# Seventy-four matmuls in the first eleven microseconds, and new scheduling constants from the end of layer 0's first pass on

## The chip, the cores and the metric

The kernel runs on one core of a Trainium2 chip. The metric is device time in microseconds for one execution, taken as the median of repeated runs. Four compute engines appear in the profile: PE (TensorE, matrix products; PEld is its weight load, which overlaps), DVE (VectorE), ACT (ScalarE) and POOL (GpSimd). SP (SyncE) issues the DMAs. Each engine works through its own list of instructions in order, and waits on semaphores for the others.

## The reference

Two layers, each a block of attention and a gated feed-forward block, with the same weights in both layers. Tokens S = 2048, model width D = 512, 32 heads of width 16, F = 1792; bfloat16 in and out.

```python
def _layernorm(x): return (x - mean(x)) / sqrt(var(x) + 1e-5)

def _A_ref(x, wqkv, wo):
    q, k, v = split_heads(x @ wqkv)              # 32 heads of 16
    p = softmax(q @ k^T * 16 ** -0.5)            # 2048 x 2048 for each head
    return merge_heads(p @ v) @ wo

def _B_ref(x, w_gate, w_up, w_down):
    return (gelu_tanh(x @ w_gate) * (x @ w_up)) @ w_down

x = A_x
x = x + _A_ref(_layernorm(x), A_wqkv, A_wo)
x = x + _B_ref(_layernorm(x), B_w_gate, B_w_up, B_w_down)
x = x + _A_ref(_layernorm(x), A_wqkv, A_wo)
x = x + _B_ref(_layernorm(x), B_w_gate, B_w_up, B_w_down)
```

## The kernel before

**Data.** All weights and the whole of x stay in SBUF. `X` is the residual in f32, 16 tiles of 128 tokens. `XNT` is the layer-normed x, transposed. `KT` holds the keys of four heads in each of 8 groups, head j on partitions 32j and up; `QT` holds queries the same way, `VP` the values with a column of ones, so that the sum of the softmax comes out of the same product as its numerator.

**Units.** The attention is cut into units: one group of four heads times a block of queries (512, in the last blocks of layer 1 also 256 or 128). A unit goes through two passes.

- Pass 1 (`p1_emit`, lines 1778 to 1816) finds the maximum of each row of scores. PE makes a tile of 128 queries by 512 keys in a PSUM bank (L1791), DVE reduces it to a maximum (L1806), one bank or two banks at a time. Some tiles are folded: PE multiplies the queries with the difference of two key blocks (L1610), ACT takes the positive part (L1617), and DVE adds and reduces in one operation (L1801), so that one DVE operation does for two tiles.
- Pass 2 (`p2_emit`, `p2_tile`, `pv_emit`) makes the scores again, transposed, with the negative maximum as an added row of `QT` (L1661). ACT takes the exponential (L1637), of one bank (128x512, called a single below) or of two (128x1024, a pair). PE then multiplies with `VP` (L1685) into bank 7, columns 0 to 271. After the last key tile ACT copies bank 7 out (L1238), and POOL or DVE normalizes.

4,096 tiles of scores go through each pass over the two layers.

**All else** (layer norms, projections, output projection, the feed-forward block; their matmuls are recorded at L717) is written as generators, "chains", which the planner steps between the matmuls of the two passes. While the gelu of a feed-forward block runs on ACT, no exponential is emitted, so that ACT changes its table only twice for a block.

**The planner.** The Python program that builds the kernel walks through simulated clocks, one for each engine (`emit`, `emit_pe`), and decides at each step which matmul PE gets next: pass 1, pass 2, a chain's step, a product of pass 2 with `VP`, or a "warm" matmul (L1830, 128x240 on zeros, into columns of bank 7 that nothing reads), which it puts in when PE's load over the last 3.4 us of its own clock falls below a bound. What it decides is a fixed list for each engine. On the chip nothing is reordered: an early or a late engine changes only how long the others wait.

**The constants.** Its decisions depend on 21 constants. They are set anew for each stretch of 16 steps of pass 1 (a step is two tiles) from the table `PLAN`, 132 rows long; a layer has 1,024 steps, so row 64 is the first of layer 1:

```python
if pos["p1"] >= STRETCH * stretch[0]:
    if stretch[0] < len(PLAN):
        SPC, SPLIT, S1C, S2C, OV, LIM, NT, P2B, LAG, LAGT, FL, GL, FX, AHD, DUE, DUEM, PIECE, GP, NPV, PB, OVF = PLAN[stretch[0]]
    stretch[0] += 1
```

For instance P2B says which banks pass 2 may take for a pair (none, 4 and 5, or 4 to 6), S1C and S2C how early the two passes are started ahead of DVE and ACT, PIECE how many matmuls of a chain go in at a time, and FL up to which lag of pass 2 tiles are folded.

**The start.** SP issues the loads: x tile 0, tiles 1 to 3, the key weights, the query weights, tiles 4 to 7, the value weights, tiles 8 to 11 and 12 to 15. POOL makes an identity matrix `IDN` (L548). DVE clears bank 7 (L558). Tiles 0 to 3 are normed by DVE, POOL and, for tile 3, ACT (`ln_fast`, `ln_a3`); each is then transposed on PE by four 128x128 matmuls with `IDN` (`transpose_tile`, L914) and copied to `XNT` by ACT (L732) or DVE (L734). Then come the first projections of the queries and keys (L717, written out by L732 and L734 and moved to `QT` and `KT` by DMA, L1072 and L1000), and with them the first tiles of pass 1. Tiles 8 to 15 are normed on ACT and POOL (`layernorm_act`): copy and sum (L886), squares (L893), normalization on POOL (L874).

```python
for i, tt in enumerate(tts):
    ...
    yield ("pe", [sk], [("XNT", tt)])
    transpose_tile(lambda ck, xs=xs: xs[:, ck * 128:(ck + 1) * 128], [sk], XNT[...], [("XNT", tt)], ...)
    xnt_rec[tt] = tag
    at["tr"] = i
```

**The end.** In the last block pass 1 is over before pass 2; the rest is exponentials, the products with `VP`, and the output projection and the feed-forward block of the last 128 tokens, of which the gated block of the 384 tokens before is partly beside it (L1363, L1389).

Of the kernel before, what the change touches and what calls it, by code (L numbers as in the profile page):

```python
# [81 lines left out]
    (0.1, 0.1, 0.55, 0.42, 0.1, -0.1, 2, 1, 70, 76, 13, 80, 0.7, 2.0, 10, 6, 2, 1, 6, 1, 0.2),  # L82
# [12 lines left out]
    (0.15, 0.1, 0.55, 0.42, 0.0, -0.05, 3, 0, 5, 76, -2, 80, 0.7, 2.0, 20, 10, 2, 1, 7, 3, 0.2),  # L95
    (0.3, 0.1, 0.55, 0.42, 0.3, -0.05, 1, 0, 30, 76, 8, 20, 0.3, 2.0, 0, 6, 1, 2, 9, 1, 0.0),
    (0.15, 0.1, 0.55, 0.42, 0.0, -0.05, 3, 0, 70, 76, -2, 80, 0.7, 2.0, 15, 2, 2, 4, 3, 4, 0.0),
    (0.2, 0.1, 0.55, 0.62, 0.3, -0.05, 1, 2, 30, 84, 8, 60, 0.3, 2.0, -5, 2, 4, 3, 9, 4, -0.05),
    (0.4, 0.4, 0.65, 0.62, 0.3, -0.05, 3, 2, 22, 76, 8, 60, 0.7, 3.5, 20, 6, 2, 4, 5, 1, 0.2),
    (0.35, 0.4, 0.65, 0.62, 0.3, -0.05, 3, 2, 22, 76, 8, 60, 0.7, 2.0, 20, 6, 2, 4, 5, 1, 0.2),  # L100
    (0.35, 0.15, 0.75, 0.12, 0.3, -0.1, 3, 0, 5, 84, 8, 60, 0.3, 1.0, 15, -6, 2, 3, 3, 1, 0.05),
    (0.2, 0.05, 0.55, 0.52, 0.3, 0.0, 2, 0, 30, 84, 8, 60, 0.3, 2.0, 0, 2, 4, 1, 7, 2, -0.05),
    (0.1, 0.05, 0.55, 0.42, 0.3, -0.05, 1, 1, 30, 100, 8, 40, 0.5, 2.0, 10, 14, 1, 2, 11, 3, -0.1),
    (0.1, 0.05, 0.55, 0.42, 0.3, -0.05, 1, 1, 30, 100, 8, 40, 0.5, 2.0, 10, 14, 1, 2, 11, 3, -0.1),
    (0.15, 0.1, 0.55, 0.42, 0.0, -0.05, 3, 0, 5, 76, -2, 80, 0.7, 2.0, 15, 10, 2, 1, 7, 3, 0.2),
    (0.15, 0.1, 0.55, 0.42, 0.0, -0.05, 3, 0, 5, 76, -2, 80, 0.7, 2.0, 15, 10, 2, 1, 7, 3, 0.2),
# [30 lines left out]
    (0.1, 0.2, 0.55, 0.52, 0.0, -0.05, 3, 0, 62, 76, -2, 80, 0.7, 2.0, 10, 2, 2, 1, 6, 3, 0.2),
    (0.1, 0.3, 0.45, 0.42, 0.1, 0.0, 2, 1, 14, 116, 13, 100, 0.3, 3.5, 0, 2, 2, 1, 7, 1, -0.05),
# [1935 lines left out]
```

## Time and profile before

| what | value |
|---|---|
| median of the runs | 2481.94 us (3 runs, 2481.69 to 2482.12) |
| the profiled execution | 2481.77 us, of which the span of its instructions 2480.0 us |
| PE busy | 2409.1 us, 97% of the span |
| DVE busy | 2382.1 us, 96% |
| ACT busy | 2331.1 us, 94% |
| POOL busy | 810.2 us, 33% |

The span runs from the first instruction to the last; 1.8 us of the execution lie outside it. Busy shares are means over stages: the first 62 us hold 10.5 us of DVE's idle time and the last 62 us hold 37.5 us, of 98 us in all. A busy PE is not PE at its peak, since warm matmuls count as work. Times in the text are counted from the start of the span.

### The profile page before, as it was taken

The page shows a single profiled execution, that of the slowest core. Times are in us where ns is not written, and L with a number is a line of the kernel's source. Part 1 is how long each engine was busy: PE and PEld are TensorE (multiplying, and loading weights), DVE is VectorE, ACT ScalarE, POOL GpSimd, SP SyncE. Part 2 cuts the span into 40 slices and gives each one's busy share as a digit, 9 for nine tenths or more (in the row PEclk, how much of TensorE's full clock was granted, in tenths as well). Part 3 has the DMA queues.
Part 4 walks back from the last instruction along what each step waited for, and adds up shares of the span by engine and source line. Part 5 has one row for each costly group of instructions (what it writes and reads, how often), then busy time and mean ns, then how long its engine had stood idle before and what let it go on. Part 6 is the DMA issues. An engine that isn't in the chain of part 4 may idle for free.

```text
span 2480.0 us, 69071 instructions
## 1 busy us (share of the span) xinstructions
PE 2409.1 (97%) x30004; PEld 1147.4 (46%) x30004; DVE 2382.1 (96%) x3173; ACT 2331.1 (94%) x3415; POOL 810.2 (33%) x1311
## 2 busy tenths in 40 slices
PE   8999999999999999999999999999999999999999
PEld 3444444444434454344434444434544345544655
DVE  8999999999999999999998999999999999999993
ACT  7999998999989999899989999989999999978987
POOL 5121125425433353521333131623116321333520
PEclk9999999999999999999999999999999999999999
DMA  3110000000000001000000000000000000000000
GB/s 94 44 57 15 2 15 12 2 2 15 13 12 2 4 11 23 6 14 11 11 10 2 9 15 5 10 16 8 4 13 15 2 10 3 14 10 12 13 8 10
DMA packets 64816, 34.32 MB, mean 14 GB/s; under 512 B 46848, under 2 KB 63488, under 8 KB 64512
## 3 DMA queue, kind: packets, MB, share of 16 engines
q1 hardware_dynamic: 64512, 29.90, 5.2%
q8 instruction: 235, 3.85, 0.6%
q14 instruction: 69, 0.57, 0.1%
HBM read 10.22 MB, written 2.10 MB: 5 GB/s over the span
## 4 chain that ended last, share of the span: by engine, by line
PE 47%; DVE 33%; ACT 19%; issue 1%; POOL 0%; ACTq 0%
DVE PM L1806 31%; ACT SCR L1637 17%; PE PS L1791 16%; PE PS L717 13%; PE PS L1685 10%; PE PS L1661 4%; PE PS L1830 4%; DVE SCR L1801 1%; ACT SCR L1617 1%; PE PS L1610 0%; PE PS L914 0%; ACT AO L1266 0%; ACT ACCS L1238 0%; ACT L1637 0%; DVE ST L769 0%
## 5 line engine op out<-in xcount | busy, mean ns | idle before, releaser
L1806 DVE TENSOR_REDUCE PM<-PS 128x1 f32<-128x512 f32 (+1 forms) x2507 | 2189.9, 935 | 47.6 <-PE PS L1661 25.1
L1637 ACT ACTIVATE SCR<-PS 128x512 bf16<-128x512 f32 (+1 forms) x2726 | 2005.9, 848 | 45.9 <-PE PS L1661 32.2
L1791 PE MATMUL PS<-KT,QT 32*128 32x512 bf16 x3894 | 1019.3, 384 | 41.3 <-DVE PM L1806 25.2
L1661 PE MATMUL PS<-QT,KT 32*128 32x512 bf16 (+2 forms) x5120 | 919.3, 340 | 2.6 <-ACT SCR L1637 1.7
L1685 PE MATMUL PS<-VP,SCR 128*128 128x51 bf16 (+1 forms) x16384 | 802.9, 187 | 10.1 <-ACT SCR L1637 5.3
L1685 PEld LDWEIGHTS PS<-VP,SCR 128*128 128x128 bf16 x16384 | 574.7, 96 | 473.4 <-issue 395.6
L1791 PEld LDWEIGHTS PS<-KT,QT 32*128 32x128 bf16 x3894 | 243.2, 91 | 526.3 <-DVE PM L1806 298.2
L1830 PE MATMUL PS<-WV,ZER 128*128 128x240 bf16 x2284 | 419.9, 265 | 3.9 <-ACT ACCS L1238 1.9
L1248 POOL TENSOR_TENSOR RL<-ACCS,CM 128x16 f32<-128x16 f32 (+2 forms) x71 | 182.2, 2567 | 485.2 <-ACT ACCS L1238 484.6
L1661 PEld LDWEIGHTS PS<-QT,KT 32*128 32x128 bf16 x5120 | 247.6, 91 | 73.9 <-ACT SCR L1637 44.3
L1830 PEld LDWEIGHTS PS<-WV,ZER 128*128 128x128 bf16 x2284 | 170.0, 96 | 70.0 <-issue 57.3
L1145 POOL TENSOR_TENSOR PM<-PM 128x16 f32<-128x16 f32 (+3 forms) x142 | 32.4, 228 | 425.0 <-DVE PM L1806 410.7
L1371 POOL TENSOR_TENSOR HT<-HT,AO 128x512 bf16<-128x512 bf16 x91 | 105.4, 1161 | 174.0 <-ACT AO L1369 174.0
L1408 POOL TENSOR_TENSOR KD<-KT 128x512 bf16<-128x512 bf16 x80 | 92.2, 1153 | 139.6 <-PE PS L1610 132.8
L1617 ACT ACTIVATE SCR<-PS 128x512 bf16<-128x512 f32 (+1 forms) x143 | 112.1, 787 | 26.3 <-PE PS L1610 25.3
L1801 DVE CUSTOM_DVE_ANT_0 SCR<-PS,SCR 128x512 bf16<-128x512 f32 x202 | 130.1, 686 | 3.2 <-PE PS L1661 1.2
L717 PE MATMUL PS<-XNT,WU 128*128 128x512 bf16 (+2 forms) x504 | 132.2, 357 | 0.0
L717 PE MATMUL PS<-WD,HT 128*128 128x512 bf16 x448 | 130.7, 381 | 0.0
L1268 POOL TENSOR_TENSOR X<-X,AO 128x512 f32<-128x512 f32 x47 | 59.5, 1266 | 199.2 <-ACT AO L1266 199.2
L717 PE MATMUL PS<-XNT,WG 128*128 128x512 bf16 (+2 forms) x504 | 119.9, 358 | 0.7 <-ACT HT L1353 0.7
L1353 ACT ACTIVATE HT<-PS 128x512 bf16<-128x512 f32 (+2 forms) x126 | 68.5, 550 | 43.1 <-PE PS L717 42.3
L717 PEld LDWEIGHTS PS<-XNT,WG 128*128 128x128 bf16 x504 | 37.6, 97 | 57.8 <-issue 33.2
(128 smaller groups left out, 1043.0 us busy)
## 6 DMA issues: line engine op xcount, KB each, us to landing
KT<-SG SPq DMA_DIRECT2D x64, 64.0 KB
QT<-MT SPq DMA_DIRECT2D x244, 1.0 KB
QT<-SG SPq DMA_DIRECT2D x56, 64.0 KB
out_dram<-AO SPq DMA_DIRECT2D x16, 128.0 KB, 1.7
WG<-in_B_w_gate_dram SPq DMA_DIRECT2D x4, 448.0 KB, 5.1
WU<-in_B_w_up_dram SPq DMA_DIRECT2D x4, 448.0 KB, 4.8
WD<-in_B_w_down_dram SPq DMA_DIRECT2D x4, 384.0 KB, 4.6
QT<-MT SPq DMA_DIRECT2D x68, 0.2 KB
```

The costliest lines, as they stand in the source:

```text
L717: ins = e.matmul(out_ap, lhsT=l, rhs=r_, start=(i == 0), stop=(i == n - 1))
L1248: emit("pool", lambda e: e.tensor_tensor(RL[:, s, 0:4 * nq], lsum, AP(CM1, 0, [[1, 128], [0, 4 * nq]]), op=ALU.pow), r=[("ACCS", s), ("CM1 ...
L1371: emit("pool", lambda e, ft=ft, o=o: e.tensor_tensor(HT[:, ft, c0:c0 + n], HT[:, ft, c0:c0 + n], AO[:, o, 0:n], op=ALU.mult), r=[("AO", o) ...
L1408: emit("pool", lambda e: e.tensor_tensor(KD[:, s, :], KT[:, g, ka * 512:(ka + 1) * 512], KT[:, g, kb * 512:(kb + 1) * 512], op=ALU.subtrac ...
L1617: emit("act", lambda e: e.activation(PT[:, s0:s0 + cnt, :], PS[:, bk:bk + cnt, :], ACTF.Relu), r=bks, w=[("PT", s0 + d) for d in range(cnt ...
L1637: emit("act", lambda e: e.activation(dst, src, ACTF.Exp, scale=DH ** -0.5), r=[BK[bk + i] for i in range(cnt)], w=[("PT", i) for i in slot ...
L1661: ins = e.matmul(bank(bk)[:, i * n:(i + 1) * n], lhsT=KT[32 * j:32 * j + 32, g, kt * 128:(kt + 1) * 128], rhs=QT[32 * j:32 * j + 32, s, 0: ...
L1685: ins = e.matmul(acc, lhsT=PT[:, slot, i * n + qt * 128:i * n + (qt + 1) * 128], rhs=AP(VP, (kt * H + 4 * g + j) * 17, [[NTT * H * 17, 128 ...
L1791: ins = e.matmul(bank(b), lhsT=QT[32 * j:32 * j + 32, s, qt * 128:(qt + 1) * 128], rhs=KT[32 * j:32 * j + 32, g, kb * 512:(kb + 1) * 512], ...
L1801: emit("dve", lambda e, i=i, b=b, sl=sl: e.tensor_tensor_reduce(PT[:, sl, :], bank(b), PT[:, sl, :], 1.0, -3.0e38, ALU.add, ALU.max, po[:, ...
L1806: emit("dve", lambda e: e.tensor_reduce(po, PS[:, bs[0]:bs[0] + cnt, :], axis=AX.X, op=ALU.max), r=bks, w=[("PM", sm) + h[1:] for h in hs] ...
L1830: return e.matmul(PS[:, b, NACC:512], lhsT=ZER[:, :], rhs=WV[:, 0, 0:512 - NACC], start=(b != 7), stop=(b != 7), skip_group_check=True)
```

## The change

Two things are changed.

First, a function `calm(n)` puts n matmuls on PE: 128x128, `IDN` times `IDN`, added to columns 272 to 399 of bank 7, which nothing reads. They are put into the list with `sch.op`, which records what they depend on (`IDN` is made, bank 7 is cleared) but moves none of the planner's clocks: the planner does not see them. 44 stand ahead of everything else on PE, then 11, 5, 9 and 5 behind the transposes of tiles 0, 1, 2 and 3.

Second, 53 of the last 72 rows of `PLAN` (between row 60 and row 130) hold other constants. Rows 0 to 59 stay. Row 128 is reached when pass 1 is over, rows 129 to 131 never.

```diff
@@ PLAN, from row 60 on (a few of the changed rows)
-    (0.1, 0.1, 0.55, 0.42, 0.1, -0.1, 2, 1, 70, 76, 13, 80, 0.7, 2.0, 10, 6, 2, 1, 6, 1, 0.2),
+    (0.1, 0.1, 0.55, 0.42, 0.1, -0.1, 2, 1, 70, 76, 13, 80, 0.7, 2.0, 10, 6, 2, 1, 5, 1, 0.1),
...
-    (0.35, 0.15, 0.75, 0.12, 0.3, -0.1, 3, 0, 5, 84, 8, 60, 0.3, 1.0, 15, -6, 2, 3, 3, 1, 0.05),
-    (0.2, 0.05, 0.55, 0.52, 0.3, 0.0, 2, 0, 30, 84, 8, 60, 0.3, 2.0, 0, 2, 4, 1, 7, 2, -0.05),
+    (0.15, 0.1, 0.55, 0.62, 0.3, -0.1, 1, 2, 22, 116, 8, 60, 0.3, 2.0, -5, 2, 4, 3, 9, 1, -0.05),
+    (0.15, 0.1, 0.55, 0.62, 0.3, -0.1, 1, 2, 22, 116, 8, 60, 0.3, 2.0, -5, -6, 4, 3, 9, 1, -0.05),
...
-    (0.1, 0.3, 0.45, 0.42, 0.1, 0.0, 2, 1, 14, 116, 13, 100, 0.3, 3.5, 0, 2, 2, 1, 7, 1, -0.05),
+    (0.2, 0.05, 0.75, 0.42, 0.3, -0.05, 2, 0, 30, 100, 8, 60, 0.3, 2.0, -5, 2, 4, 3, 7, 1, -0.05),
@@ _build(...)
-           ... T_TP=0.7, T_TPI=2.0, VL=0):
+           ... T_TP=0.7, T_TPI=2.0, VL=0, HC=(44, 11, 5, 9, 5)):
@@ behind the setup of KBIAS
+        def calm(n):
+            for _ in range(n):
+                sch.op("pe", lambda e: e.matmul(PS[:, 7, NACC:NACC + 128], lhsT=IDN[:, :], rhs=IDN[:, :],
+                                                start=False, stop=False, skip_group_check=True),
+                       r=[("IDN",)], w=[BK[7]])
+
+        calm(HC[0])
         filled = set()
@@ ln_to_xnt
                 xnt_rec[tt] = tag
                 at["tr"] = i
+                if tag == ("in", 0) and tts[0] == 0:
+                    calm(HC[i + 1])
```

In the two built programs the lists compare as follows. Apart from the 74, PE's list is the same up to the 1,923rd matmul of pass 1 of 3,894; DVE's up to its 1,517th reduction of 2,507, ACT's up to its 1,592nd exponential of 2,726.

| instruction | before | after |
|---|---|---|
| ACT exponential, pair / single (L1637) | 1370 / 1356 | 1394 / 1308 |
| ACT positive part of a fold, pair / single (L1617) | 59 / 84 | 58 / 88 |
| DVE reduction, two banks / one (L1806) | 1185 / 1322 | 1179 / 1330 |
| DVE add and reduce of a fold (L1801) | 202 | 204 |
| PE pass 1 / folds (L1791 / L1610) | 3894 / 202 | 3892 / 204 |
| PE warm matmuls (L1830) | 2284 | 2286 |
| PE silent matmuls | 0 | 74 |
| POOL memsets for folds, two columns / one (L1620) | 59 / 84 | 58 / 88 |
| SP DMAs | 667 | 667 |

All other instructions stand in both lists in the same number.

More of the change, by code (lines that the diff above doesn't have):

```diff
@@ L317, in _build @@
 def _build(nc, x_in, wqkv, wo, wg, wu, wd, out, layer_blocks=((512, 512, 512, 512), (512, 512, 512, 256, 128, 128)), ffn_groups=((512, 512, 512, 512), (512, 512, 512, 384, 128)),
[L318 removed]
+           n_ahead=6, n_pre=6, S1C=0.45, S2C=0.42, OV=0.3, PD=80, FDUE=20, LIM=-0.05, NT=1, AHD=2.0, DUEM=2, FDL2=0, OPD=12, URG=0.3, ft_tok=512, n_pt=8, n_qt=8, SPLIT=0.15, SPC=0.1, PVC=47, WARM=0.55, WARML=0.42, NPV=7, BOOST=0.0, LAG=62, LAGT=84, GP=2, SING=0, DUE=0, END=360, LAGE=10, FD=205, FDL=-10, QD=32, KD_=16, VD=20, FL=8, FMAX=6, NKD=2, FLOOK=2, FX=0.3, GF=1, NSPL=5, HSPL=0, TSPL=1, HNA=3, TNA=3, PB=1, OVF=0.0, FNP=1, NSG=3, LNT=8, HV=16, TW=0.95, HF=60, VS=14, SO=1.0, SF=1, SP=0, FAST=1, P2B=1, PIECE=2, GL=60, GLE=20, HARD=-1e9, VPARK=60, RUSH=1, XL=1000, NFE=2, NFA=6, LM1=0, T0=0.6, A3=1, DTX=2, DTA=2, T_TP=0.7, T_TPI=2.0, VL=0, HC=(44, 11, 5, 9, 5)):
     S = x_in.shape[1]
```

1 line of the change is left out of this document (removed), and 98 rows, old and new, of the table PLAN.

## The prediction

> **What bounds the kernel now.** I read the page's head and its chain of waits first, then the busy time of the engines in stretches, then the start and the tail as timelines.
>
> ```profile
> PE 2409.1 (97%) x30004; PEld 1147.4 (46%) x30004; DVE 2382.1 (96%) x3173; ACT 2331.1 (94%) x3415; POOL 810.2 (33%) x1311
> PE 47%; DVE 33%; ACT 19%; issue 1%; POOL 0%; ACTq 0%
> ```
>
> Three engines are full at once. PE's 97% holds warm matmuls, so it is the least certain of the three; DVE and ACT carry work that has to be done, and the chain changes hands between all three. So time can only go where DVE or ACT stands still, or where their own work shrinks. The built lists tell where the change acts at all: apart from the silent matmuls the first 1,923 pass 1 matmuls are in the old order, and the reordered places, found by counting pass 1 matmuls into the trace of before, are these stretches:
>
> ```profile
> core 0: us, PE busy (x) PEld busy (x) DVE busy (x) ACT busy (x) POOL busy (x), PEclk, DMA share, GB/s
> 1189.00:1209.00 20.00, 19.52 (x277) 10.09 (x274) 19.66 (x26) 19.84 (x22) 2.58 (x7) 1.00 0.05 10
> 1479.00:1549.00 70.00, 68.37 (x904) 34.87 (x901) 68.95 (x105) 69.24 (x79) 12.91 (x28) 1.00 0.02 4
> 1618.00:1658.00 40.00, 38.89 (x273) 12.96 (x272) 39.67 (x66) 32.24 (x52) 12.22 (x35) 1.00 0.06 12
> 1846.00:1924.00 78.00, 75.67 (x933) 36.22 (x929) 77.29 (x107) 74.07 (x112) 44.68 (x72) 1.00 0.11 22
> 1968.00:2061.00 93.00, 91.22 (x1134) 41.18 (x1130) 91.71 (x111) 89.42 (x156) 26.36 (x34) 1.00 0.02 8
> 2178.00:2197.00 19.00, 18.61 (x107) 6.31 (x104) 18.98 (x20) 8.00 (x14) 4.91 (x12) 1.00 0.05 10
> 2249.00:2315.00 66.00, 64.02 (x946) 32.72 (x945) 63.55 (x80) 60.65 (x98) 20.48 (x45) 1.00 0.04 12
> 2391.00:2427.00 36.00, 34.30 (x404) 17.91 (x403) 34.70 (x50) 26.03 (x42) 4.82 (x9) 1.00 0.03 5
> ```
>
> The third pair of numbers is DVE. It is idle for 0.34 + 1.05 + 0.33 + 0.71 + 1.29 + 0.02 + 2.45 + 1.30 = 7.49 us in these 422 us. That is all that a better order could win from DVE there. The kernel's larger idle stretches (the start, and the tail behind 2427 us) are looked at below.
>
> **The change part by part: the silent matmuls.** The start, by the timeline:
>
> ```profile
> 1.10 0.29 POOL L548 TENSOR_SCALAR_AFFINE_SELECT IDN<-HT 128x128 bf16<-128x128 bf16 x1
> 0.97 0.48 DVE L558 MEMSET PS<- 128x512 f32 x1 [0.97 <-PEq L2059]
> 3.91 2.53 SPq L508 DMA_DIRECT2D HT<-in_A_x_dram  x2
> 6.45 0.61 PE L914 MATMUL PS<-IDN,XN 128*128 128x128 bf16 x4 [6.45 <-DVE XN L790]
> 11.24 1.86 PE L717 MATMUL PS<-XNT,WQ 128*128 128x512 bf16 x4 [0.56 <-issue]
> 13.14 0.60 ACT L732 ACTIVATE SG<-PS 128x512 bf16<-128x512 f32 x1 [3.25 <-PE PS L717]
> 13.64 0.62 ACT L886 ACTIVATE X<-HT 128x512 f32<-128x512 bf16 x1
> 14.85 0.69 DVE L734 CAST SG<-PS 128x512 bf16<-128x512 f32 x1 [1.70 <-PE PS L717]
> 16.32 1.42 PEld L717 LDWEIGHTS PS<-XNT,WQ 128*128 128x128 bf16 x7 [0.28 <-issue]
> 20.16 1.82 DVE L1806 TENSOR_REDUCE PM<-PS 128x2 f32<-128x1024 f32 x2
> 30.53 3.01 POOL L874 TENSOR_SCALAR ATT<-HT,ACCS 128x512 bf16<-128x512 bf16 x4 [0.18 <-POOL ACCS L900]
> 33.92 6.71 DVE L1806 TENSOR_REDUCE PM<-PS 128x2 f32<-128x1024 f32 x8 [3.02 <-PE PS L1791]
> ```
>
> The column of the granted clock says 1.00 all along, but the pace doubles: the four query matmuls take 1.86 us, (1.86 - 0.17) / 4, some 0.43 us each, while from 16.32 us seven weight loads follow each other in 1.42 us, 0.20 us apart. PE is slow until it has worked without a break for 5 us.
>
> Can the 44 run in the gap? They need `IDN` (1.10 + 0.29 = 1.39 us) and bank 7 (0.97 + 0.48 = 1.45 us). At the slow pace 128 columns take a quarter of 0.43, 0.107 us, so they end at 1.45 + 44 x 0.107 = 6.16 us, 0.29 us ahead of the first transposes at 6.45. Bounds: if they follow each other as slowly as the four transposes on the mean (0.61 / 4 = 0.152), they end at 8.14 and the transposes are 1.7 us late. The other 30 stand in gaps between the transposes. Of the two I take the 0.107, since the four transposes include one latency at their end.
>
> What a fast PE wins: four transposes at 0.39 in place of 0.61 (the 0.39 is the row of the same four at 18.07 us, below) twice on the path, 0.4 us, the four query matmuls 4 x 0.21 = 0.9, the four key matmuls 0.9. ACT could write out the query projection at 13.14 - 1.3 = 11.8, DVE the key projection at 14.85 - 2.2 = 12.7, and the first reductions come some 2.2 to 2.7 us sooner.
>
> ```profile
> 18.07 0.39 PE L914 MATMUL PS<-IDN,XN 128*128 128x128 bf16 x4
> HT<-in_A_x_dram SPq DMA_DIRECT2D x2, 512.0 KB, 9.5
> 28.21 0.77 POOL L874 TENSOR_SCALAR ATT<-HT,ACCS 128x512 bf16<-128x512 bf16 x1 [0.37 <-ACT ATT L893]
> 20.00:22.00 2.00, 2.00 (x18) 1.31 (x17) 2.00 (x4) 2.00 (x7) 0.87 (x2) 1.00 0.46 98
> 26.00:28.00 2.00, 1.88 (x9) 0.43 (x8) 2.00 (x4) 2.00 (x8) 1.52 (x2) 1.00 0.03 8
> ```
>
> What is late next: at 33.92 us DVE stands still for 3.02 us in any case, waiting for keys of tiles 8 to 15, which come through ACT's copies and squares (from 13.64 on) and POOL's normalization (28.21, which waits for ACT, to 33.54). And the first of these copies cannot start sooner than its data: issued at 3.91, landed 9.5 us later, at 13.4. ACT has no gap from there to the normalization (its busy time, the fourth number, is 2.00 of 2.00 us in these two windows as in those between). So of the 2.2 to 2.7 us ACT's chain wins 13.64 - 13.4 = 0.2 us; the rest becomes a longer wait of DVE before 33.92. I take **-0.2 us**. Ends: -2.7 (if the wait at 33.92 shortened as well), and above zero +0.7, the 1.7 us of late transposes less the 1.0 us or more that the fast matmuls behind them give back.
>
> [...]
>
> **The new constants.** The durations by form:
>
> ```profile
> L1637 ACT ACTIVATE SCR<-PS 128x1024 bf16<-128x1024 f32 x1370 | 1297.9, 1074 | 20.6 <-PE PS L1661 14.7
> L1637 ACT ACTIVATE SCR<-PS 128x512 bf16<-128x512 f32 x1356 | 726.6, 619 | 25.3 <-PE PS L1661 17.5
> L1617 ACT ACTIVATE SCR<-PS 128x1024 bf16<-128x1024 f32 x59 | 62.1, 1059 | 2.0 <-PE PS L1610 1.6 <-DVE PM L1801 0.4
> L1617 ACT ACTIVATE SCR<-PS 128x512 bf16<-128x512 f32 x84 | 50.1, 597 | 24.2 <-PE PS L1610 23.7
> L1806 DVE TENSOR_REDUCE PM<-PS 128x2 f32<-128x1024 f32 x1185 | 1433.6, 1218 | 35.2 <-PE PS L1661 18.1 <-PE PS L1791 5.9 <-PE PS L1610 0.2
> L1806 DVE TENSOR_REDUCE PM<-PS 128x1 f32<-128x512 f32 x1322 | 887.5, 681 | 12.3 <-PE PS L1661 7.1 <-PE PS L1791 1.3
> L1801 DVE CUSTOM_DVE_ANT_0 SCR<-PS,SCR 128x512 bf16<-128x512 f32 x202 | 130.1, 686 | 3.2 <-PE PS L1661 1.2 <-PE PS L1791 0.6 <-PE PS L1610 0.2
> L1801 DVE DVE_READ_ACCUMULATOR2_ANT PM<- 128x1 f32 x202 | 16.7, 83 | 0.0
> ```
>
> ACT: 48 single exponentials become 24 pairs, 24 x (2 x 0.619 - 1.074) = 3.9 us less; the folds' positive parts cost 4 x 0.597 - 1.059 = 1.3 us more; together 2.6 us less. DVE: 8 x 0.681 - 6 x 1.218 + 2 x (0.686 + 0.083) = -0.3 us, which is nothing. PE: two more warm matmuls, in idle time. POOL's memsets and its moved key difference, and SP's moved DMAs (two transposes of the attention output go ahead of two query moves, three groups of query moves and one store of the output change places) lie on engines that are a third busy or wait most of the time; without that cover a moved query transfer would hold up its unit by one issue, and no group of these is larger than four.
>
> Of the new pairs seven fall at about 2058 us, seven at about 2298 and two net behind 2424. Is ACT the one that DVE waits for there?
>
> ```profile
> DVE PM L1806 <- PE PS L1661: 5.2, 20, 0.4
> DVE PM L1806 <- PE PS L1791: 0.7, 2, 0.5
> ```
>
> Between 2178 and 2427 us DVE's reductions wait 5.2 us for a PE that stands in front of a pass 2 matmul, so for a bank that ACT has not emptied. There a shorter exponential helps DVE. I let the 2.1 us that ACT saves outside the tail pass through and round: **-2.0 us** for 1189 to 2427. The far ends: -7.5, all idle time of DVE in the eight stretches; and above, +8: if all 422 us ran at the idle share of the worst of them, 2249 to 2315 (2.45 of 66, 3.7%), DVE would be idle for 15.6 us in place of 7.5.
>
> The tail, behind the last pass 1 work, is ACT's:
>
> ```profile
> 2421.80 5.83 ACT L1637 ACTIVATE SCR<-PS 128x512 bf16<-128x512 f32 x10
> 2438.19 7.54 ACT L1637 ACTIVATE SCR<-PS 128x1024 bf16<-128x1024 f32 x8
> ```
>
> A single takes 0.58 us here, a pair 0.94. Behind the last gelu the old list has 20 singles and 30 pairs, the new one 16 and 32: 2 x (2 x 0.58 - 0.94) = 0.4 us less. 272 pass 2 matmuls in place of 276 are left behind the last matmul of pass 1, one tile. Together **-0.5 us**, ends 0 and -1.0. The new list ends in more singles (six singles and three pairs for the last twelve tiles, before two and five), which costs 0.4 us at the very end if PE is ready; it is in the count.
>
> Sum: -0.2 - 2.0 - 0.5 = -2.7. The profiled execution took 2481.77, so 2479.1; the median of the runs lies 0.17 above it: **2479.2 us**, 0.11% less.
>
> **The rivals.**
> 1. *Nothing.* DVE is full wherever the order changes (98.2% of the 422 us), ACT's savings become ACT's waits: within 0.5 us of 2481.9. For it: the idle shares; against: the 20 waits on pass 2.
> 2. *The new order fills DVE's idle time.* 5.5 of the 7.5 us, with start and tail as above: 2481.9 - 6.2 = 2475.7. For it: the waits there are short and many (20 of at most 0.4 us), as a wrong order leaves them. Against: in half of the stretches there is under 0.8 us to win.
> 3. *The start passes through.* 2.7 us sooner at the first reductions and all later: 2479.2 - 2.5 = 2476.7. Against: the landing at 13.4 us. [...]
> 4. *Slower: a pair keeps two banks for longer.* The pass 1 matmul or chain step behind it on PE waits for both halves: 1.074 - 0.619 = 0.46 us later for each of 24 pairs, 10.9 us at most. Nothing shows beside the savings until a quarter of them hold up DVE (2.7 us), and it is slower by over 0.2%, about what a measurement of this kernel tells from no change (5.0 us), from 17 of them on. With 20: +9.1 - 2.7, 2488. Against: the kernel has 1370 pairs as it is, and its reductions wait 18.1 + 7.1 us for pass 2 over all 2480 us. The bound of +8 above gives about the same.
>
> **How the numbers follow.** Forecast (2477 to 2481): 0.46. Nothing: 0.22. Filled: 0.17. Start: 0.06, half of it beyond 2477. Slower: 0.09. So faster by over 0.2% 0.17 + 0.03 = 0.20, slower 0.09, within 0.71. The range leaves out rival 4 and the deep end of rival 2 (0.05): 2475 to 2484. The likeliest case alone is 2477 to 2481.
>
> **What would show it.** In the new profile: PE busy from 1.5 us on, the four query matmuls in about 1.0 us in place of 1.86 and ACT's write-out at about 12 us; ACT's first copy of tile 8 still at 13.4 us and a wait of DVE before 33.7 us of more than 4 us. Busy ACT 2.6 us less. DVE's reductions at about 2295 us 2 us sooner, their waits on pass 2 behind 2178 us down to some 3 us; the last pass 2 work 2.7 us sooner. I am wrong if the reductions at 34 us come 1 us or more sooner (the start passes through), or if they come later than 33.9, or if a stretch of the eight grows.

## The result, and the profile after

The changed kernel takes 2477.28 us (median of 16 runs, 2476.78 to 2478.8), the kernel before, timed beside it, 2481.94 us (16 runs, 2480.72 to 2482.69). The ratio is 0.9982, with an interval of 0.9975 to 0.999: 4.66 us or 0.19% less, a small gain that the interval tells from none. The profiled execution took 2477.07 us, its span 2475.3 us, 4.7 us less than before. In some executions (e4, e6 and e8 below) the granted clock falls to 0.50 for one stretch of 3.4 us, which costs 1.3 to 1.4 us; where a profile below holds such a stretch, it is said.

Line numbers have moved: by 7 between the lines 570 and 970 of before (L717 is now L724), by 9 behind that (L1806 is L1815, L1637 is L1646, L1661 is L1670). The silent matmuls are L572.

The page of the changed kernel, its head and the first line of its chain:

```profile
span 2475.3 us, 69012 instructions
PE 2387.4 (96%) x29880; PEld 1152.7 (47%) x30080; DVE 2381.7 (96%) x3179; ACT 2328.4 (94%) x3394; POOL 810.3 (33%) x1314
PE 48%; DVE 32%; ACT 19%; issue 1%; POOL 0%; DMA 0%; ACTq 0%
```

DVE has as much work as before, ACT 2.7 us less. (PE's 30,080 weight loads stand beside 29,880 matmuls: 200 matmul records are missing from this trace, so PE's busy time is not to be compared.) The start of the changed kernel, as a timeline (start, duration, then the idle time before and what ended it):

```profile
1.54 4.85 PE L572 MATMUL PS<-IDN 128*128 128x128 bf16 x44 [1.54 <-DVE PS L558]
6.10 0.41 DVE L797 TENSOR_SCALAR XN<-SCR,MV,LNS 128x512 bf16<-128x512 bf16 x1
6.57 0.47 PE L921 MATMUL PS<-IDN,XN 128*128 128x128 bf16 x4 [0.18 <-DVE XN L797]
11.34 0.81 PE L724 MATMUL PS<-XNT,WQ 128*128 128x512 bf16 x3 [0.50 <-issue]
11.98 1.03 PE L724 MATMUL PS<-XNT,WK 128*128 128x512 bf16 x4
12.18 0.60 ACT L739 ACTIVATE SG<-PS 128x512 bf16<-128x512 f32 x1 [2.38 <-PE PS L724]
12.68 0.62 ACT L893 ACTIVATE X<-HT 128x512 f32<-128x512 bf16 x1
HT<-in_A_x_dram SPq DMA_DIRECT2D x2, 512.0 KB, 8.8
17.53 1.81 DVE L1815 TENSOR_REDUCE PM<-PS 128x2 f32<-128x1024 f32 x2
31.66 4.99 DVE L1815 TENSOR_REDUCE PM<-PS 128x2 f32<-128x1024 f32 x6 [3.09 <-PE PS L1800]
```

The 44 end at 6.39 us and the transposes start at 6.57, right behind the normalization that they wait for anyway. The projections run at the fast pace (four key matmuls in 1.03 us). The first reductions come at 17.53 (before 20.16), and those at 33.92 now come at 31.66 us, with a wait of 3.09 us ahead of them, which was 3.02.

The eight reordered stretches of the changed kernel, each shifted by the lead that it has there (the columns are those of the table for before):

```profile
1189.00:1209.00 20.00, 19.18 (x278) 10.31 (x277) 19.94 (x27) 19.84 (x23) 0.86 (x1) 1.00 0.03 7
1476.00:1546.00 70.00, 67.46 (x903) 34.32 (x899) 69.55 (x106) 69.70 (x80) 13.45 (x31) 1.00 0.02 4
1615.00:1655.00 40.00, 39.06 (x269) 13.02 (x273) 39.71 (x66) 32.01 (x51) 12.38 (x35) 1.00 0.07 15
1843.00:1921.00 78.00, 75.91 (x931) 37.10 (x935) 77.19 (x113) 74.99 (x113) 44.72 (x75) 1.00 0.11 21
1966.00:2059.00 93.00, 89.82 (x1136) 42.16 (x1145) 91.77 (x112) 88.55 (x148) 26.35 (x34) 1.00 0.03 7
2176.00:2195.00 19.00, 18.34 (x92) 5.97 (x91) 18.89 (x19) 8.13 (x13) 3.77 (x9) 1.00 0.02 3
2247.00:2313.00 66.00, 64.13 (x965) 32.68 (x971) 64.07 (x81) 60.21 (x84) 22.18 (x50) 1.00 0.05 13
2387.00:2423.00 36.00, 34.49 (x411) 18.34 (x412) 34.74 (x50) 26.25 (x39) 4.82 (x9) 1.00 0.04 6
```

DVE is idle for 0.06 + 0.45 + 0.29 + 0.81 + 1.23 + 0.11 + 1.93 + 1.26 = 6.14 us here, 1.35 less than before, and nearly half of that is in the second stretch (1.05 to 0.45). Its waits from 2174 to 2423 us (total, times, longest), and ACT's two forms of exponential and the last of them:

```profile
DVE PM L1815 <- PE PS L1670: 4.5, 17, 0.4
DVE PM L1815 <- PE PS L1800: 1.0, 3, 0.5
...
L1646 ACT ACTIVATE SCR<-PS 128x1024 bf16<-128x1024 f32 x1394 | 1321.8, 1079 | 22.5 <-PE PS L1670 17.0
L1646 ACT ACTIVATE SCR<-PS 128x512 bf16<-128x512 f32 x1308 | 702.2, 622 | 23.1 <-PE PS L1670 16.1
...
2448.29 5.87 ACT L1646 ACTIVATE SCR<-PS 128x512 bf16<-128x512 f32 x9
```

The last exponential ends at 2448.29 + 5.87 = 2454.16 us; before it ended at 2459.02. Between the two ends, the lead over the kernel before can be followed by counting: the time at which the n-th of the 4,096 pass 1 tiles is reduced on DVE, in us against before. Both tiles of a fold are counted, since the two lists have their folds at different places.

| landmark | before | after | silent alone (e1) | silent, three rows (e10) | silent, rows from 92 (e6) |
|---|---|---|---|---|---|
| 18th tile | 35.1 | -2.3 | -2.3 | -2.4 | -2.4 |
| 1984th | 1151.2 | -2.2 | -2.3 | -2.5 | -2.3 |
| 2496th | 1477.3 | -2.3 | -2.3 | -2.5 | -2.3 |
| 2640th | 1554.9 | -3.2 | -2.2 | -3.3 | -2.3 |
| 3136th | 1838.2 | -3.3 | -2.3 | -3.3 | -2.3 |
| 3360th | 1958.8 | -3.6 | -2.3 | -3.3 | -2.6 |
| 3744th | 2195.4 | -3.6 | -2.2 | -3.3 | -1.2 (behind a stretch of slow clock) |
| 3920th | 2312.1 | -4.1 | -2.2 | -3.3 | -1.6 |
| last of pass 1 | 2426.9 | -4.1 | -2.2 | -3.3 | -1.7 |
| last exponential | 2459.0 | -4.9 | -2.2 | -3.3 | -2.4 |
| span | 2480.0 | -4.7 | -2.2 | -3.3 | -2.2 |

So the 4.7 us are 2.3 from the first 35 us, 0.9 from the stretch at 1480 to 1550, 0.4 from there to 1960, 0.5 from 2195 to 2312, and 0.6 from the tail. The lead grows where the order differs, and is kept in between.

### The profile page after: what moved, and what is told of

It reads as the page before. It is cut to its first block, busy times and chain, and to the rows that moved or that the text cites. A ratio compares the mean times of both kernels' runs of the same rounds, so it can differ in the third digit from the quotient of the medians.

```text
span 2475.3 us, 69012 instructions
## 1 busy us (share of the span) xinstructions
PE 2387.4 (96%) x29880; PEld 1152.7 (47%) x30080; DVE 2381.7 (96%) x3179; ACT 2328.4 (94%) x3394; POOL 810.3 (33%) x1314
## 4 chain that ended last, share of the span: by engine, by line
PE 48%; DVE 32%; ACT 19%; issue 1%; POOL 0%; DMA 0%; ACTq 0%
DVE PM L1815 30%; ACT SCR L1646 17%; PE PS L1800 15%; PE PS L724 13%; PE PS L1694 11%; PE PS L1670 4%; PE PS L1839 4%; DVE SCR L1810 1%; ACT SCR L1626 1%; PE PS L1619 0%; ACT AO L1275 0%; PE PS L921 0%; ACT AO L1378 0%; ACT L1646 0%; ACT HT L1362 0%
## 5 line engine op out<-in xcount | busy, mean ns | idle before, releaser
L1815 DVE TENSOR_REDUCE PM<-PS 128x1 f32<-128x512 f32 (+1 forms) x2509 | 2188.7, 934 | 47.0 <-PE PS L1670 24.0
L1646 ACT ACTIVATE SCR<-PS 128x1024 bf16<-128x1024 f32 (+1 forms) x2702 | 2003.7, 858 | 45.6 <-PE PS L1670 33.0
L1670 PE MATMUL PS<-QT,KT 32*128 32x512 bf16 (+2 forms) x5120 | 915.8, 340 | 3.3 <-ACT SCR L1646 2.1
L1670 PEld LDWEIGHTS PS<-QT,KT 32*128 32x128 bf16 x5120 | 246.8, 91 | 76.7 <-ACT SCR L1646 47.4
L1626 ACT ACTIVATE SCR<-PS 128x512 bf16<-128x512 f32 (+1 forms) x146 | 113.7, 782 | 26.8 <-PE PS L1619 26.0
L724 PE MATMUL PS<-XNT,WU 128*128 128x512 bf16 (+2 forms) x449 | 120.3, 354 | 5.8 <-issue 3.7
L724 PE MATMUL PS<-WD,HT 128*128 128x512 bf16 x387 | 116.3, 380 | 6.5 <-issue 4.9
L724 PE MATMUL PS<-XNT,WG 128*128 128x512 bf16 (+2 forms) x490 | 116.3, 357 | 2.4 <-issue 1.4
L724 PEld LDWEIGHTS PS<-XNT,WG 128*128 128x128 bf16 x504 | 37.7, 97 | 58.2 <-issue 32.9
```

The costliest lines, as they stand in the source:

```text
L724: ins = e.matmul(out_ap, lhsT=l, rhs=r_, start=(i == 0), stop=(i == n - 1))
L1626: emit("act", lambda e: e.activation(PT[:, s0:s0 + cnt, :], PS[:, bk:bk + cnt, :], ACTF.Relu), r=bks, w=[("PT", s0 + d) for d in range(cnt ...
L1646: emit("act", lambda e: e.activation(dst, src, ACTF.Exp, scale=DH ** -0.5), r=[BK[bk + i] for i in range(cnt)], w=[("PT", i) for i in slot ...
L1670: ins = e.matmul(bank(bk)[:, i * n:(i + 1) * n], lhsT=KT[32 * j:32 * j + 32, g, kt * 128:(kt + 1) * 128], rhs=QT[32 * j:32 * j + 32, s, 0: ...
L1815: emit("dve", lambda e: e.tensor_reduce(po, PS[:, bs[0]:bs[0] + cnt, :], axis=AX.X, op=ALU.max), r=bks, w=[("PM", sm) + h[1:] for h in hs] ...
```

## The experiments

**e1: the silent matmuls alone.** Does the start pass through?

```diff
 the changed kernel, with all of PLAN as before
-    (0.1, 0.1, 0.55, 0.42, 0.1, -0.1, 2, 1, 70, 76, 13, 80, 0.7, 2.0, 10, 6, 2, 1, 5, 1, 0.1),
+    (0.1, 0.1, 0.55, 0.42, 0.1, -0.1, 2, 1, 70, 76, 13, 80, 0.7, 2.0, 10, 6, 2, 1, 6, 1, 0.2),
...
```

> The 74 silent matmuls with the old constants; the work of every engine is else in the old order. Theory of the prediction (A: ACT's copies of x tiles 8 to 15 set the reductions at 33.9 us): 0.2 to 1.0 us sooner than before, since ACT's first copy came at 12.68 in place of 13.64 in the changed kernel. Rival (B: the first reductions set it, through PE's fixed order): the 2.3 us that the changed kernel showed at 34 us belong to this part alone, so span 2480.0 - 2.3 = 2477.7, constant from 34 us to the end.

Measured: 2479.88 us (11 runs, 2479.53 to 2481.41) against 2481.48 (33 runs, 2480.53 to 2482.83), ratio 0.9995 [0.9987, 1.0004]; span 2477.8, 2.2 less. The timeline of e1:

```profile
12.65 0.63 ACT L893 ACTIVATE X<-HT 128x512 f32<-128x512 bf16 x1
31.65 4.99 DVE L1815 TENSOR_REDUCE PM<-PS 128x2 f32<-128x1024 f32 x6 [3.12 <-PE PS L1800]
```

What follows: the reductions of 33.92 are 2.3 us sooner, and the table shows the lead kept, at -2.2, to the last instruction. Nothing behind 34 us waits for a fixed time. The silent matmuls are worth 2.2 us in this trace and 1.6 in the medians. The medians alone would not settle it, since their interval includes 1.

**e2: the constants alone.**

```diff
 the changed kernel, without calm
-        calm(HC[0])
-                if tag == ("in", 0) and tts[0] == 0:
-                    calm(HC[i + 1])
```

> The new constants without the silent matmuls. If the two parts add up, span 2480.0 - 2.4 = 2477.6 (the prediction had -2.5 for this part): nothing gained before 1190 us, 1.1 us by 1850 us, the largest step between 2270 and 2430 us. If the constants only pay with the earlier start, less than 1 us.

Measured: 2478.70 us (11 runs, 2478.04 to 2480.58), ratio 0.999 [0.9981, 0.9999]; span 2476.5, 3.5 less. In this execution PE became fast some 2 us sooner than in the profiled execution of before, though nothing was changed there, and its first reductions come at 19.08 us against 20.16. That lead of 1.1 us stays until 1230 us. So the constants win 3.5 - 1.1 = 2.4 us in the traces, 2.8 in the medians. With e1: 2.2 + 2.4 = 4.6 of 4.7 us by traces, 1.6 + 2.8 = 4.4 of 4.66 by medians. The two parts add.

**e3: only the 44 silent matmuls ahead, none in the gaps.** Are the other 30 needed?

```diff
-HC=(44, 11, 5, 9, 5)
+HC=(44, 0, 0, 0, 0)        (and PLAN as before)
```

> Old constants, the 44 matmuls ahead of the first transposes alone, without the 30 between the transposes. If the 44 open the clock and the transposes and projections keep it open: like the 74, span 2477.7. If the clock closes in the gaps between the transposes: the four query matmuls at some 0.43 us each again, first reduction at about 20 us, span 2479.5 to 2480.

Measured: 2481.59 us (10 runs, 2480.88 to 2482.46), 1.0001 [0.9992, 1.001]; span 2479.2. The stretches of e3 (columns as above; the last three are the granted clock, the DMA share and GB/s), and the query matmuls in its timeline:

```profile
4.50:7.80 3.30, 1.46 (x23) 1.11 (x22) 3.02 (x11) 3.04 (x7) 1.75 (x4) 1.00 1.10 363
7.95:14.60 6.65, 5.15 (x21) 2.10 (x19) 3.40 (x9) 3.10 (x9) 5.40 (x11) 0.50 0.83 264
14.80:18.20 3.40, 3.32 (x23) 1.75 (x22) 3.04 (x8) 3.40 (x11) 0.47 (x1) 1.00 0.44 95
...
11.04 1.86 PE L724 MATMUL PS<-XNT,WQ 128*128 128x512 bf16 x4 [0.56 <-issue]
```

What follows: the 44 do open the clock, at 4.48 us (they take 4.00 us here, 4.85 in the changed kernel), but PE is busy for only 1.46 of the next 3.30 us, and the clock is at 0.50 again until 14.7 us, over the projections (1.86 us as before). The 30 matmuls in the gaps are what keeps it open in these profiles: in that of e8, which has them, the clock opened as early (4.56 us) and stayed open, with PE busy for 2.11 of the next 3.30 us; in that of the changed kernel it opened at 6.75 us, with PE busy for 2.47 of the next 3.30 us, and was open over the projections. How much work in the gaps is enough is not shown.

**e4: what sets the reductions at 33.92?** The prediction took them to hang on ACT's copies of tiles 8 to 15, and these on the landing of x. In the kernel before, the last two loads of x change places on SP's queue, so that tiles 8 to 11 land later.

```diff
+        sp = sch.streams["sp"]
+        i2 = [i for i, o in enumerate(sp) if o.grp == "ldx2"][0]
...
+        sp[i2], sp[i2 + 1] = sp[i2 + 1], sp[i2]
```

> The kernel before, with the loads of x tiles 8 to 11 and 12 to 15 issued in the other order: ACT's first copy of tile 8 can start at about 14.9 us in place of 13.64. Theory A: the reductions of 33.92 us come 1.2 us later and the span is 1.2 us longer. Theory B (PE stands behind pass 1 matmuls that wait for DVE, and ACT has slack there): the reductions stay within 0.4 us of 33.9 and the span within 0.5 us of 2480.0.

Measured: 2481.92 us (10 runs, 2481.11 to 2482.49), 1.0002 [0.9993, 1.0011]. The timeline of e4:

```profile
13.28 1.45 PE L717 MATMUL PS<-XNT,WK 128*128 128x512 bf16 x4
14.25 0.63 ACT L886 ACTIVATE X<-HT 128x512 f32<-128x512 bf16 x1
19.25 1.81 DVE L1806 TENSOR_REDUCE PM<-PS 128x2 f32<-128x1024 f32 x2
33.25 3.24 DVE L1806 TENSOR_REDUCE PM<-PS 128x2 f32<-128x1024 f32 x4 [3.12 <-PE PS L1791]
```

The profiled span, 2480.8 us (mean granted clock 0.999), holds a stretch at half clock at 2345 us that costs 1.4 us, so neither theory can be read from it. The copy starts 0.6 us later than before (14.25, 13.64). The reductions do not: they come 0.7 us sooner (33.25, 33.92). What did come sooner is the first reductions (by 0.9 us: 19.25, 20.16), because PE became fast at 14.14 us in this execution, in the middle of the key matmuls. So in the kernel before the reductions at 33.92 follow the first reductions and not ACT's copies. The order of PE's list fits that: pass 1 matmuls that wait for DVE stand ahead of the projections of later keys.

But 0.2 of the 0.9 us are lost again by 33.25, and that is ACT's chain. Ahead of the reductions stand transposes on PE, and ahead of these ACT writes out a projection of the values (`VP`), behind its copies and squares. Before, ACT waits there for PE; in e4 and in the changed kernel PE waits for ACT (first line before, then e4, then after):

```profile
30.99 0.60 ACT L736 ACTIVATE VP<-PS 128x512 bf16<-128x512 f32 x1 [0.58 <-PE PS L717]
32.04 0.24 PEld L914 LDWEIGHTS PS<-IDN,ATT 128*128 128x128 bf16 x4 [0.40 <-ACT VP L736]
30.45 0.24 PEld L921 LDWEIGHTS PS<-IDN,ATT 128*128 128x128 bf16 x4 [0.37 <-ACT VP L743]
```

Two chains meet, and the later one decides. In the profiles of before, e2 and e3 the reductions come 13.8 us behind the first reductions. In those of the changed kernel, e1 and e4 (and of e5 to e8 and e10) they come 19.0 us behind the first copy, and more than 13.8 behind the first reductions. For the copy at 13.64 the second chain ends at 32.6 us, so before it had 1.3 us of slack.

**e5 and e6: which constants?** The silent matmuls stay; new constants below row 92 only, and from row 92 on only.

```diff
 e5: PLAN[92:] as before          e6: PLAN[:92] as before
```

> Silent matmuls, new constants up to row 91 (about 1810 us), old ones from row 92 on. If the constants' gain is made where the traces first part, the silent kernel's span of 2477.8 falls by the 1.1 us that the changed kernel had won by then, and keeps it to the end: 2476.7. If most is made behind 2270 us and does not need the first rows, the span stays within 1.2 us of 2477.8. An order that no longer fits the later constants could lose some us.

> Silent matmuls, old constants up to row 91, new ones from row 92 on. If the gain of the later rows (2.5 - 1.1 = 1.4 us by the traces) stands by itself: 2477.8 - 1.4 = 2476.4. If it needs the earlier rows: about 2477.8 or more.

Measured: e5 2478.43 us (10 runs, 2478.25 to 2479.94), 0.9988 [0.9978, 0.9997], span 2476.7; e6 2478.15 (10 runs, 2477.84 to 2479.51), 0.9986 [0.9977, 0.9996], span 2477.8; before beside them 2481.68. Against e1's span e5 is 1.1 us shorter, but 0.2 of it were there at 1478 us, from a start that ran a little sooner; the rows win 0.9. The profiled execution of e6 holds a stretch at half clock (stretches of e6):

```profile
2156.50:2159.90 3.40, 2.78 (x42) 1.24 (x40) 3.18 (x7) 3.40 (x7) 2.27 (x4) 1.00 0.21 39
2159.95:2163.30 3.35, 3.10 (x39) 1.79 (x36) 2.79 (x5) 2.09 (x5) 3.11 (x5) 0.50 0.00 0
2163.40:2166.80 3.40, 3.40 (x49) 1.58 (x48) 2.55 (x4) 3.00 (x7) 1.03 (x3) 1.00 0.21 43
```

The clock is at 0.50 for one stretch, and the landmarks jump by 1.4 us there. Less that, its span would be 2476.4, 1.4 less than e1. So the rows below 92 win 0.9 and those from 92 on 1.4 us, 2.3 together, nearly the difference between e1 and the changed kernel (2477.8 - 2475.3 = 2.5).

**e7 and e8: what is a pair of exponentials worth?** The prediction valued each of the new pairs at 0.164 us. The changed kernel, with 16 pairs at 2062 to 2077 us (e7), or at 2276 to 2292 us (e8), done as two singles each. Everything else, banks and waits too, stays.

```diff
-            emit("act", lambda e: e.activation(dst, src, ACTF.Exp, scale=DH ** -0.5),
+            halves = [(dst, src)]
+            if cnt == 2 and 2 * pos["p2"] >= 3420 and n_split[0] < 16:      (e8: 3780)
+                n_split[0] += 1
+                halves = [(PT[:, slots[i], :], bank(bk + i)) for i in range(2)]
+            ... e.activation(d, s, ACTF.Exp, scale=DH ** -0.5) for each
```

> The changed kernel with 16 pairs of exponentials at about 2062 to 2077 us done as two singles each on ACT, all else in the same order: 16 x (2 x 0.619 - 1.074) = 2.6 us more of ACT, which is busy for 30.0 of 30 us there. Theory of the prediction (what ACT saves passes through where DVE waits for pass 2): pass 1 from 2100 us on and the end 1.5 to 2.6 us later. Rival (ACT's savings become ACT's waits, DVE sets the pace): under 0.5 us.

> The same with 16 pairs at about 2276 to 2292 us, where ACT is busy for 28.4 of 30 us and DVE for 29.5: 2.6 us more of ACT. If it is the fuller engine that decides, less passes through than at 2060 us: 0.5 to 1.5 us at the end. If savings on ACT pass through everywhere: 2.6 us.

Measured: e7 2478.12 us (10 runs, 2477.77 to 2479.54), 0.9986 [0.9977, 0.9996], span 2476.4; e8 2478.86 (10 runs, 2477.68 to 2479.61), 0.9987 [0.9978, 0.9997], span 2477.3. The page of e7, and one stretch of e8:

```profile
PE 2388.9 (96%) x29880; PEld 1152.9 (47%) x30080; DVE 2381.7 (96%) x3179; ACT 2329.6 (94%) x3410; POOL 810.2 (33%) x1314
```

```profile
2342.75:2346.05 3.30, 3.30 (x49) 2.02 (x49) 2.24 (x4) 2.53 (x3) 2.17 (x3) 0.50 0.07 10
```

In e7 ACT is busy for 1.2 us more (2329.6, 2328.4), and the end comes 1.1 us later. So ACT's time does pass through there, whole. But the 16 pairs cost 1.2 / 16 = 0.075 us each, under half of the 0.164. The trace of before shows that exponentials that follow each other on ACT overlap, so that the sum of their durations is more than the time that they take: pairs in a row, of 1.074 us each, start 0.920 us apart on the mean, and singles, of 0.619, 0.497, and 2 x 0.497 - 0.920 = 0.074. In e8 ACT is busy for 1.3 us more (2329.7, 2328.4); the lead shrinks by 0.8 us at the split pairs, so less passes through there, and by another 1.3 behind the stretch at 0.50 shown, which has nothing to do with the edit.

**e9: more silent matmuls ahead.** PLAN as before, 64 in place of 44.

```diff
-HC=(44, 11, 5, 9, 5)
+HC=(64, 11, 5, 9, 5)
```

> The silent kernel (old constants) with 64 in place of 44 matmuls ahead of the first transposes. In the changed kernel the 44 end at 6.39 us and tile 0 is normed at 6.51: 0.1 us of cover. The 20 more take 20 x 0.056 = 1.1 us at the fast pace, 20 x 0.107 = 2.1 us at the slow one, so the first transposes start 1.0 to 2.0 us late. If the path from the first transposes on sets the first reduction: 1.0 to 2.0 us of the 2.3 are lost, span 2478.8 to 2479.8. If there is slack behind the first transposes (tile 3 is the last to be normed): under 0.5 us is lost.

Measured: 2480.22 us (10 runs, 2479.51 to 2486.23), 0.9999 [0.999, 1.0008] against 2481.42; span 2478.2, 0.4 more than e1. The timeline of e9:

```profile
1.54 5.61 PE L572 MATMUL PS<-IDN 128*128 128x128 bf16 x64 [1.54 <-DVE PS L558]
6.99 0.39 PE L921 MATMUL PS<-IDN,XN 128*128 128x128 bf16 x4
```

The 64 end at 7.15 us by the row and hold the transposes back by half a microsecond: `XN` is ready at 6.4. That is less than the 1.0 to 2.0 us expected, since the clock opened at 5.52 us in this execution and the last of the 64 ran at the fast pace. The first reductions are 0.3 us later than in e1 and the end 0.4, so nothing of the delay is given back. That it alone makes the 0.4 is not shown: the reductions at 34 us come 0.6 us later, and the chain of waits ahead of them leads through a transfer of keys (`KT`, 3.38 us) that does not stand in it before.

**e10: three rows of the constants.** e5's gain lies between 1478 and 1550 us. The silent matmuls, and new constants in rows 78 to 80 alone.

```diff
+    (0.15, 0.1, 0.55, 0.62, 0.3, -0.1, 1, 2, 22, 116, 8, 60, 0.3, 2.0, -5, 2, 4, 3, 9, 1, -0.05),
+    (0.15, 0.1, 0.55, 0.62, 0.3, -0.1, 1, 2, 22, 116, 8, 60, 0.3, 2.0, -5, 2, 4, 3, 9, 1, -0.05),
+    (0.15, 0.1, 0.55, 0.62, 0.3, -0.1, 1, 2, 22, 116, 8, 60, 0.3, 2.0, -5, -6, 4, 3, 9, 1, -0.05),
```

> Silent matmuls, old constants but for rows 78 to 80. Counts of instructions on DVE and ACT stay; two folds' ACT operations come two exponentials later, and matmuls on PE change places between 1480 and 1550 us. The changed kernel won 0.6 us over the silent one by 1481 us and 0.9 us by 1558 us, while DVE's idle time there fell from 1.05 to 0.45 us in 67. If the mere order wins it: span 2477.8 - 0.9 = 2476.9, kept to the end. If the gain needs fewer or cheaper instructions: 2477.8.

Measured: 2478.53 us (10 runs, 2478.30 to 2478.72), 0.999 [0.998, 0.9999]; span 2476.7, 1.1 less than e1, as e5. The stretches of e1, then those of e10:

```profile
1478.00:1500.00 22.00, 21.19 (x286) 11.33 (x284) 21.52 (x32) 21.62 (x26) 4.78 (x5) 1.00 0.01 2
1500.00:1545.00 45.00, 44.24 (x585) 22.16 (x582) 44.43 (x67) 44.63 (x52) 7.84 (x20) 1.00 0.02 5
```

```profile
1478.00:1500.00 22.00, 20.90 (x284) 10.50 (x284) 21.88 (x32) 21.98 (x25) 4.78 (x5) 1.00 0.01 2
1500.00:1545.00 45.00, 43.87 (x592) 22.61 (x590) 44.67 (x66) 44.73 (x52) 7.86 (x20) 1.00 0.02 5
```

The heads of the pages of e1 and e10:

```profile
PE 2412.9 (97%) x30078; PEld 1152.7 (47%) x30078; DVE 2382.3 (96%) x3173; ACT 2330.8 (94%) x3415; POOL 810.1 (33%) x1311
PE 2384.9 (96%) x29866; PEld 1151.0 (46%) x30071; DVE 2381.5 (96%) x3173; ACT 2330.5 (94%) x3415; POOL 811.3 (33%) x1311
```

On DVE, ACT and POOL no instruction is added or left out against e1. PE's order from 1480 to 1550 us differs, two folds on ACT come two exponentials later, and one small transpose on DVE changes places with a reduction. On PE there are seven weight loads fewer (30,078, 30,071): by the trace seven warm matmuls, all between 1461 and 1540 us. DVE's idle time there falls from 0.48 + 0.57 = 1.05 to 0.12 + 0.33 = 0.45 us. By the landmarks the lead over e1 grows from 0.2 us ahead of the stretch to 1.1 behind it, so the three rows win 0.9 us, the whole of e5's gain; the idle time explains 0.6 of it, and the rest was not traced. It is a gain without less work on DVE or ACT. Whether the order makes it, or PE's seven warm matmuls fewer (by the row of ten in 1.20 us at 17.27 us of the changed kernel some 0.1 us each), no run separates.

**e11: a denser PE in the gaps.** The changed kernel with more silent matmuls behind the transposes.

```diff
-HC=(44, 11, 5, 9, 5)
+HC=(44, 14, 9, 17, 10)
```

> The changed kernel with 14, 17 and 10 in place of 11, 9 and 5 silent matmuls behind the transposes of tiles 0, 2 and 3, and 9 in place of 5 behind tile 1, to fill the rest of PE's gaps. If the clock sometimes closes in these gaps, the median falls by some tenths and the spread of 2.0 us gets smaller. If the gaps are closed enough as it is: the same within 0.3 us. If the added matmuls run at the slow pace in some executions they delay a transpose, at most 0.5 us.

Measured: 2476.96 us (11 runs, 2476.76 to 2478.71), 0.9984 [0.9975, 0.9992] against 2481.42; span 2475.2. It beats the kernel before; from the changed kernel (0.9982 [0.9975, 0.999], span 2475.3) it can't be told apart, and its spread is no smaller (2.0 us). So more matmuls in the gaps win nothing that shows.

## Why the prediction was right, and where its working was not

The time lies inside the forecast's band (2477 to 2481, measured 2477.28), the gain is within the 0.2% called no change, and the sign is right. It lies 0.3 us from the band's edge, and that it is inside is luck as much as working: the sum was too small by 2.0 us (2.7 predicted, 4.66 measured), and nearly all of that is one step.

**The silent matmuls' own cost: right.** 44 in 4.85 us are 0.110 us each (0.107 predicted), the end is at 6.39 (6.16), no transpose is late, the write-out on ACT comes at 12.18 (about 12), the key matmuls take 1.03 us.

**The failing step: "So of the 2.2 to 2.7 us ACT's chain wins 13.64 - 13.4 = 0.2 us; the rest becomes a longer wait of DVE before 33.92."** Measured: -2.3 us at 35 us and -2.2 at the end (e1), in place of -0.2, and a wait of 3.09 us in place of over 4. The prediction's own sign of being wrong, reductions at 34 us that come 1 us or more sooner, is there. Two things were wrong in it. The step took ACT's chain for the last one ahead of 33.92 and put its slack at nothing; it had 1.3 us of slack, and the first reductions and PE's list, which is in order, came last (e4). And the landing at 13.4 us was taken from one execution as fixed; in the changed kernel and in e1 the copies start at 12.68 and 12.65, 1.0 us sooner than before, and the transfer's row says 8.8 us in place of 9.5. What was right is that ACT's chain is the next to be late: in the changed kernel it decides, and the reductions win 2.3 of the 2.6 us that the first reductions won (e4's third line: PE waits 0.37 us for ACT). Rival 3 (the start passes through), given 0.06, is what happened to the start, less 0.4 us. Rival 1 (nothing) and rival 4 (slower) did not occur.

**The end -2.7 / +0.7 of that term: right as bounds.** The upper one counted on late transposes being partly given back; in e9 first reductions 0.3 us later go with an end 0.4 us later. With the 74 the clock was open in time: in the eight profiles with the 74 or more whose trace records the clock, it opened between 4.6 and 7.3 us (6.75 in the changed kernel, 5.52 in e9), each time ahead of the projections (from 11.04 us on in e1, 11.57 in e9).

**The constants: -2.5 predicted, -2.4 to -2.5 measured (e1, e2), in part for another reason.** Between 35 us and the last pass 1 reduction the lead grows by 4.1 - 2.3 = 1.8 us (2.0 predicted), and in the tail by 4.9 - 4.1 = 0.8 up to the last exponential, 0.6 up to the end of the span (0.5 predicted). But 0.9 of this come from three rows which change no count on DVE and ACT (e10); the forecast had put that stretch at nothing and the whole saving on ACT's pairs. DVE's idle time falls there, which is rival 2's mechanism; over the eight stretches it falls by 1.35 us, a quarter of that rival's 5.5. That a better order does it is argued: the seven warm matmuls fewer are the other candidate, and the prediction had such matmuls "in idle time".

e7 confirms that ACT's time passes through behind 2060 us, as argued, but at 0.075 us a pair and not 0.164, so the term "24 x (2 x 0.619 - 1.074)" was over twice too large: 24 x 0.075 = 1.8 us. The group of all exponentials on the two pages agrees with the smaller one:

```profile
L1637 ACT ACTIVATE SCR<-PS 128x512 bf16<-128x512 f32 (+1 forms) x2726 | 2005.9, 848 | 45.9 <-PE PS L1661 32.2
L1646 ACT ACTIVATE SCR<-PS 128x1024 bf16<-128x1024 f32 (+1 forms) x2702 | 2003.7, 858 | 45.6 <-PE PS L1670 33.0
```

2.2 us less, where the prediction counted 3.9. That ACT's whole busy time fell by 2.7 us, as predicted (2.6), is thus in part luck: the folds' positive parts took 1.6 us more, and no other group fell by more than 0.1 us. The rows of groups overlap each other, so they do not add up to the engine's busy time, and where the rest of the 2.7 lies they do not say.

Nor is the 1.4 us of the rows from 92 on shown to be the pairs' work. Counted in the two traces, one of the 24 new pairs stands between 1840 and 1930 us, seven between 2000 and 2060, fourteen (not seven) between 2250 and 2320, and two behind. The lead grows by 0.3 us with the one (1838 to 1959 us in the table), by nothing with the seven, by 0.5 with the fourteen, and by 0.6 in the tail. Around the seven ACT is idle for 4.45 of 93 us, before 3.58, and DVE for 1.23, before 1.29: what ACT saved there became ACT's own wait, as rival 1 had it. So the price of a pair where ACT is full (e7) is not what a saved pair wins elsewhere.

**The waits on pass 2: right in direction only.** Behind 2178 us they fell from 5.2 to 4.5 us and not to 3, as a smaller gain per pair would have it.

## What to carry to other kernels

A wait that looks fixed by a transfer near it has to be followed back through the queue of the engine that the wait names, the slack of each chain that ends there worked out, and the transfer's landing compared over more than one execution, before a gain ahead of it is written off. The price of two instructions against one on the same engine comes from the spacing of their starts or from an experiment: the difference of mean durations overstates it where neighbours overlap (0.164 against 0.075 us). Where two versions are compared by counting, everything that does the counted work has to be in the count. Filling PE's idle start with harmless work paid here only where the filling reached over the gaps too: 44 matmuls alone opened the clock at 4.48 us, it was at 0.50 again from 7.95 us on, and they won nothing that the measurement shows (ratio 1.0001).

## What the runs showed of the hardware that was not expected

The moment at which PE becomes fast varies between executions of the same start: 16.36 us in the profiled execution of before, 14.14 in e4, with the first reductions at 20.16 and 19.25 us. In e4 that is 2.5 us after the first projection matmul (11.62), in before 5.1, so the prediction's 5 us without a break are what the one trace of before shows and no rule. A part of the spread of the kernel before can come from this, and the silent matmuls are worth 2.2 us against one execution, 1.2 to 1.3 against the traces of e2 and e3, and 1.6 in the medians.

In three of the profiles the clock fell to 0.50 for one stretch deep in the kernel: at 2160 us (e6), 2343 us (e8) and 2345 us (e4), each for some 3.4 us (3.35 us at 0.50 are shown above for e6, 3.30 for e8), each costing 1.3 to 1.4 us. The runs of e5 fit it: seven lie at 2478.3 to 2478.7 us with a mean granted clock of 1.000, three at 2479.7 to 2479.9 with 0.999. PE was not idle ahead of it in e6: in the stretch before the one at 0.50, shown above, it was busy for 2.78 of 3.40 us. Nor does that share alone bring the fall about, since the same stretch of e7 has as little work on PE and no fall of the clock behind it:

```profile
2156.50:2159.90 3.40, 2.78 (x41) 1.24 (x39) 3.18 (x7) 3.40 (x7) 2.23 (x4) 1.00 0.20 37
2159.95:2163.30 3.35, 3.19 (x54) 1.77 (x50) 3.14 (x6) 3.01 (x7) 3.11 (x6) 1.00 0.01 2
```

What decides it stays open. The column of the granted clock also reads 1.00 over the first microseconds, in which the pace is half: in before it reads 1.00 from the start, while four query matmuls take 1.86 us (1.02 in e1), and the first change of the clock is recorded at 16.36 us. Ahead of that it says nothing.
